# First Fourier stage of the kernels moved into the phases' two banks and ahead of a chunk's sums, in a fused S4D + GLU kernel

## The chip, the cores and the metric

The kernel runs on one core of a Trainium2 chip. A core has TensorE (PE, matmuls), VectorE (DVE), ScalarE (ACT), GpSimd (POOL) and SyncE (SP, which here only starts transfers). Each takes its instructions in the order of its own list, and semaphores make an instruction wait for another engine or for a transfer. The metric is the device time of one execution in microseconds (us); lower is better. Matmul results stand in PSUM, which the program treats as eight banks of 2 KB per partition.

## What is computed

Layer norm of `A_u` (2048 tokens, 448 channels), then two branches added to `A_u`: a state-space convolution over the tokens and a gated MLP (the GLU).

```
xn = layernorm(A_u)
# A: long convolution, one kernel of 2048 taps per channel, built from 256 modes
K  = 2 * Re( sum_n C[d,n] * exp(A[d,n] * dt[d] * l) )          # l = 0..2047
yA = irfft(rfft(K, 4096) * rfft(xn, 4096))[:2048] + xn * D_skip
# B: GLU with sigmoid gate, F = 1792
yB = (sigmoid(xn @ w_gate) * (xn @ w_up)) @ w_down
out = A_u + yA + yB
```

## The kernel before

The program is two Python generators that emit instructions in turn. `glu()` (L731) emits the GLU: for each of 14 blocks of 128 hidden features and each 512 tokens, two groups of 11 gate matmuls (`gate`, L697, matmuls at L710) into PSUM tiles named `gu`, and then the down projection (L831) into tiles `po`. Every operand is split into a high and a low part, so one product is three matmuls. `gu` and `po` tiles come from one pool, `psg`, which hands out four banks in rotation (`tag="gu", bufs=4`). I call gate and down matmuls together the GLU matmuls. The first half of the tokens goes through all blocks, then the second half; between them stand transposes of the second half's tokens, which also use `gu` tiles (the crossing).

`conv()` (L1067) emits the convolution. After a preparation, `kgen` (L455) builds the 448 kernels' values in 56 chunks of 8 channels (NCK = 56), and then `spectra` (L855) does the frequency-domain product and the way back. One chunk `cn` of `kgen` is:

- `ahead(cn + 1)` (L528): two PE matmuls (L535) put the next chunk's phases into `tr`, a PSUM tile of two banks with one buffer; four ACT activations (L543 to L546) turn them into sines and cosines `S` (two buffers).
- `magnitudes` (L490), once per two chunks (a pair): 11 POOL products (L501, L513) into `me` and `mf` (two buffers each); `squares` (L522) on ACT finishes them.
- three DVE products (L603, L604 into `Et`, two buffers; L605 into `Ft`, one buffer).
- the chunk's sums (L619): 32 PE matmuls of `Ft` with `Et` into `ko`, a bank with one buffer that collects four chunks. After the fourth chunk a small matmul (L629) adds the skip term and ACT copies `ko` to `ks` in SBUF (L632).
- the first Fourier stage, `first_stage` (L549), once per four chunks: 32 PE matmuls (L561) of `ks`, even ones into the bank `kp`, odd ones into `kq`. `kp` is a bank of the convolution's pool; `kq` is a bank of the GLU's rotation. Two ACT copies (L567) and a transfer (L568) send the result to DRAM. It is emitted behind the sums of the third chunk of the next four.

So PSUM holds `gu`/`po` x4, `tr` x2, `ko`, `kp`: eight banks. A scheduler of the framework orders each engine's list from the emitted program. `tc.issue_after(glu_mm[0].ins)` puts the sums and the first stage behind the GLU matmul that was emitted last before them. Nothing puts a GLU matmul behind a chunk but the rotation of the four banks, whose third party is `kq`. In `spectra`, from its first step on, GLU matmuls are also put behind the convolution's (`sp_mm`).

Of the kernel before, what the change touches and what calls it, by code (L numbers as in the profile page):

```python
# [11 lines left out]
F32 = mybir.dt.float32  # L12
# [25 lines left out]
HP = 300  # L38
# [14 lines left out]
NCK = D // DC  # L53
# [74 lines left out]
def s4d_glu_kernel(ctx, tc, io):  # L128
    nc = tc.nc
    hp = tc.high_priority  # L130
# [46 lines left out]
    psg = ctx.enter_context(tc.tile_pool(name="psg", bufs=1, space=PSUM))  # L177
# [277 lines left out]
    def kgen(pk):  # L455
# [93 lines left out]
        def first_stage(bank):  # L549

            ks, sk = tl["ks"], tl["sk"].rearrange("p k (s r j) -> p r k s j", r=2, j=2)

            pss = [
                psc[-1].tile([128, 8, 2, 32], F32, name="kp", bufs=1),
                psg.tile([128, 8, 2, 32], F32, name="kq", tag="gu", bufs=4),
            ]
            for s_ in range(8):
                for c in range(2):
                    for r in range(2):
                        rows = slice(64 * r, 64 * r + 64)  # L560
                        nc.tensor.matmul(  # L561
                            pss[r][64 * c : 64 * c + 64, s_].rearrange("p j k -> p (j k)"),
                            ks[rows, s_], wk[rows, c], start=True, stop=True,
                            skip_group_check=True,
                        )
            for r in range(2):
                nc.scalar.copy(sk[:, r], pss[r].rearrange("p s j k -> p k s j"))  # L567
            nc.scalar.dma_start(  # L568
                sk_d[bank // 7, :, :, bank % 7].rearrange("k p c -> p k c"),
                tl["sk"].rearrange("p (k i) c -> p k (i c)", i=4),  # L570
            )
# [11 lines left out]
        for g in range(NCK // NCH):  # L583
            for c in range(NCH):
                cn = g * NCH + c
# [23 lines left out]
                    mags = coming  # L609
                yield WK / 3  # L610
                if cn % 4 == 0:
                    ko = psc[-1].tile([128, 8, 64], F32, name="ko", bufs=1)
                with tc.issue_after(glu_mm[0].ins):
                    for q in range(2):
                        sl = 2 * (cn % 4) + q
# [15 lines left out]
                    )  # L631
                    nc.scalar.copy(ks.rearrange("p s (q b) -> p s q b", q=2), ko.rearrange("p s (b q) -> p s q b", q=2))  # L632
                yield WK / 3
                if cn % 4 == 2 and cn > 3 or cn + 1 == NCK:

                    with hp(HP) if cn + 1 == NCK else tc.issue_after(glu_mm[0].ins):
                        first_stage((cn - 3) // 4 if cn + 1 < NCK else cn // 4)

    def w_load(f, raw=None, eng=nc.sync):
        fs = slice(128 * f, 128 * f + 128)  # L640
# [426 lines left out]
    def conv():  # L1067
        with tc.tile_pool(name="psk", bufs=1, space=PSUM) as ps_, tc.tile_pool(
# [79 lines left out]
            with tc.tile_pool(name="pk", bufs=1, side="right", reuse_waits="tile") as pk:  # L1148
                yield from kgen(pk)
# [8 lines left out]
    lasts, glu_mm, sp_mm, glu_on, outs, x1s, hfs, xls = [], [], [], [], [0], [0], [], []  # L1158
    xq, psc, raws, acl, marks, slots, pqs = list(x_first), [], [], [], [None, None], {}, []
# [44 lines left out]
```

## Time and profile before

| | us |
|---|---|
| median of 3 runs | 746.65 (744.72 to 747.68) |
| the profiled execution | 741.93, of which its span is 740.1 |
| PE busy | 668.2 (90%) |
| DVE busy | 587.9 (79%) |
| ACT busy | 420.6 (57%) |
| POOL busy | 420.8 (57%) |
| granted PE clock, mean | 0.949 |

Busy is the time in which an engine had an instruction running. The clock is the share of full speed that TensorE was granted, so a busy PE at a low clock does less. Matmul rows overlap, since matmuls are pipelined: the distance between starts, not the length of a row, is what one costs. A matmul of 32-bit operands that the program writes as one instruction can stand in the trace as two (the 32 matmuls of a chunk's sums as x64). A row of the chain or of the waits names the waiting instruction, an arrow, and what it waited for.

### The profile page before, as it was taken

To read this page: it belongs to the slowest core of one execution; us is meant where nothing else is said; L and a number is where in the kernel's file an instruction comes from. 1 tells how busy PE (TensorE), PEld (TensorE's weight loads), DVE (VectorE), ACT (ScalarE), POOL (GpSimd) and SP (SyncE) were. 2 spreads that over 40 slices of the span, in tenths; PEclk is the share of its full clock that TensorE was granted. 3 is DMA by queue.
4 is the path that set the end of the run, shared out by engine and by line. 5 is a ranking of instruction groups with operands and counts; after the bars stand their busy time and mean duration, and the time that the engine had idled before them with its cause. 6 is when DMAs were issued, how large, how long until landed. Compare 5 with 4: busy or idle time off the path is not lost.

```text
span 740.1 us, 20863 instructions
## 1 busy us (share of the span) xinstructions
PE 668.2 (90%) x8581; PEld 515.1 (70%) x8581; DVE 587.9 (79%) x779; ACT 420.6 (57%) x651; POOL 420.8 (57%) x453
## 2 busy tenths in 40 slices
PE   2998999988999999788999999999988999788976
PEld 1765878866877787555878888888765667466655
DVE  5799998699999999886679898886757777756833
ACT  3655454689778789887387777777323322222310
POOL 2120116869999999974645776765537773541301
PEclk9999999995999999999999999999998989898987
DMA  9935338451313564354863323322669887874464
GB/s 199 235 114 198 116 102 263 147 188 58 126 48 97 175 191 116 114 181 148 264 188 99 93 95 95 99 81 83 157 171 266 222 244 185 262 210 130 125 169 132
DMA packets 94335, 114.47 MB, mean 155 GB/s; under 512 B 13728, under 2 KB 83936, under 8 KB 93984
## 3 DMA queue, kind: packets, MB, share of 16 engines
q1 hardware_dynamic: 72512, 92.54, 43.1%
q10 hardware_dynamic: 19248, 14.91, 7.0%
q0 software_dynamic: 2480, 5.67, 3.0%
q8 instruction: 68, 1.11, 0.6%
q14 instruction: 27, 0.22, 0.1%
HBM read 68.32 MB, written 44.76 MB: 153 GB/s over the span
## 4 chain that ended last, share of the span: by engine, by line
PE 40%; POOL 19%; issue 11%; DVE 11%; DMA 11%; SPq 5%; ACT 3%; POOLq 0%; DVEq 0%; ACTq 0%
PE gu L710 17%; PE po L831 10%; POOL me L513 7%; PE ko L619 5%; POOL mf L513 5%; PE tr L535 2%; DMA v_d<-vt 2%; POOL dl L796 2%; DVE Ft L605 2%; DVE Et L604 1%; DMA skl<-sk_d 1%; SPq L896 1%; DMA xe<-in_A_u_dram 1%; DVE Et L603 1%; POOL yy L934 1%
## 5 line engine op out<-in xcount | busy, mean ns | idle before, releaser
L513 POOL TENSOR_TENSOR me<-me,pm 128x32 f32<-128x32 f32 (+1 forms) x168 | 149.5, 890 | 67.6 <-DVE Et L604 57.8
L513 POOL TENSOR_TENSOR mf<-mf,pm 128x64 f32<-128x64 f32 (+1 forms) x112 | 118.8, 1061 | 5.3
L710 PE MATMUL gu<-xh,wh 128*128 128x512 f32 x336 | 103.2, 415 | 3.0 <-ACT th L718 1.2
L710 PE MATMUL gu<-xl,wh 128*128 128x512 f32 x336 | 97.7, 394 | 0.0
L710 PE MATMUL gu<-xh,wl 128*128 128x512 f32 x336 | 96.5, 395 | 0.0
L604 DVE TENSOR_TENSOR Et<-me,S 128x1024 f32<-128x1024 f32 x56 | 80.4, 1436 | 13.9 <-ACT me L526 9.0
L831 PE MATMUL po<-dh,hh 128*128 128x448 f32 (+1 forms) x227 | 87.4, 385 | 0.8 <-DVE acc L836 0.8
L605 DVE TENSOR_TENSOR Ft<-mf,S 128x1024 f32<-128x1024 f32 x56 | 83.8, 1496 | 5.1 <-PE ko L619 3.2
L831 PE MATMUL po<-dh,hl 128*128 128x448 f32 (+1 forms) x227 | 84.5, 374 | 2.0 <-DVE hl L728 2.0
L831 PE MATMUL po<-dl,hh 128*128 128x448 f32 (+1 forms) x227 | 84.8, 374 | 0.2 <-POOL dl L796 0.2
L603 DVE TENSOR_TENSOR Et<-me,S 128x1024 f32<-128x1024 f32 x56 | 77.5, 1385 | 4.0 <-ACT S L546 3.5
L710 PEld LDWEIGHTS gu<-xh,wh 128*128 128x128 f32 x336 | 62.6, 195 | 25.8 <-issue 6.9
L543 ACT ACTIVATE S<-tr 128x1024 f32<-128x1024 f32 x56 | 57.9, 1033 | 34.4 <-PE tr L535 18.7
L619 PEld LDWEIGHTS ko<-Et,Ft 128*32 128x32 f32 x3584 | 56.0, 114 | 28.0 <-issue 10.5
L619 PE MATMUL ko<-Et,Ft 128*32 128x64 f32 x3584 | 66.0, 227 | 9.7 <-DVE Ft L605 5.3
L710 PEld LDWEIGHTS gu<-xh,wl 128*128 128x128 f32 x336 | 63.8, 191 | 14.9 <-DVE hl L728 0.7
L710 PEld LDWEIGHTS gu<-xl,wh 128*128 128x128 f32 x336 | 63.0, 189 | 14.8 <-issue 1.4
L726 ACT CAST hh<-gu 128x512 fp32r<-128x512 f32 x56 | 33.1, 591 | 69.8 <-DVE gu L721 68.8
L836 DVE SCALAR_TENSOR_TENSOR acc<-po,acc 128x448 f32<-128x448 f32 (+1 forms) x81 | 48.7, 613 | 28.2 <-PE po L831 27.9
L934 POOL TENSOR_TENSOR yy<-yy 128x448 f32<-128x448 f32 (+1 forms) x16 | 28.5, 1778 | 67.1 <-DVE yy L931 66.9
L546 ACT ACTIVATE S<-S,hpi 128x1024 f32<-128x1024 f32 x56 | 65.6, 1171 | 0.0
L718 ACT ACTIVATE th<-gu 128x512 f32<-128x512 f32 x56 | 33.9, 606 | 43.5 <-PE gu L710 43.5
(214 smaller groups left out, 1346.7 us busy)
## 6 DMA issues: line engine op xcount, KB each, us to landing
sk_d<-sk ACTq DMA_DIRECT2D x14, 512.0 KB
sx<-x_d SPq DMA_DIRECT2D x64, 112.0 KB
skl<-sk_d SPq DMA_DIRECT2D x64, 112.0 KB
v_d<-vt SPq DMA_DIRECT2D x27, 224.0 KB
vp<-v_d SPq DMA_DIRECT2D x6, 896.0 KB
wt_d<-wh SPq DMA_DIRECT2D x9, 512.0 KB
wt_d<-wl SPq DMA_DIRECT2D x9, 512.0 KB
wl<-wt_d SPq DMA_DIRECT2D x9, 512.0 KB
```

What stands on the lines that cost most here:

```text
L513: ins = nc.gpsimd.tensor_tensor(m[:, :, w + a : 2 * w : n], m[:, :, a:w:n], par(base + i).unsqueeze(2).to_broadcast([128, 4 * DC, w // n]) ...
L543: nc.scalar.activation(rows(cs), pv, AF.Abs)
L546: sins[:] = [nc.scalar.activation(cs, cs, AF.Sin, scale=-TWO_PI, bias=hpi)]
L603: v.tensor_tensor(Et[:, :, :, 32:64], two(me[:, :, 32:64]), S[:, 1::-1], ALU.mult)
L604: v.tensor_tensor(Et[:, :, :, 0:32], two(me[:, :, 0:32]), S[:, 1:3, :, ::-1], ALU.mult)
L605: fts[:] = [v.tensor_tensor(Ft, two(mf), S[:, 3:5], ALU.mult)]
L619: nc.tensor.matmul(ko[32 * j : 32 * j + 32, sl], Ft[:, cc, DC * h + 4 * q + j], Et[:, cc, DC * h + 4 * q + j], start=(k == 0), stop=(k == ...
L710: glu_mm[:] = [nc.tensor.matmul(ps, a_, b_, start=(n == 0), stop=(n == len(mm) - 1))]
L718: marks[0] = nc.scalar.activation(th, pgu[0], AF.Tanh, scale=0.5)
L831: glu_mm[:] = [nc.tensor.matmul(po[:, ds], a_[:, bs], w_[:, ds], start=(n == 0), stop=(n == 3 * fc - 1))]
L836: v.scalar_tensor_tensor(acc[:, b, ds], po[:, ds], 0.5, acc[:, b, ds], ALU.mult, ALU.add)
L934: eng.tensor_tensor(yy[:, :, 0], yy[:, :, 0], yy[:, :, 1], ALU.subtract)
```

## The change

`kq` is gone. The first stage writes its two halves to the two banks of a `tr` tile, the tile of the phases. The sums of every second group of four chunks go to the bank `kp` instead of `ko`, so the copy of one group and the sums of the next use different banks. And the first stage is emitted ahead of the third chunk's sums, no longer behind them; the one after the last chunk stays where it was.

```
-            pss = [
-                psc[-1].tile([128, 8, 2, 32], F32, name="kp", bufs=1),
-                psg.tile([128, 8, 2, 32], F32, name="kq", tag="gu", bufs=4),
-            ]
+            both = psc[-1].tile([128, 2, 512], F32, name="tr", bufs=1)
+            pss = [both[:, r].rearrange("p (s j k) -> p s j k", s=8, j=2) for r in range(2)]
...
                 if cn % 4 == 0:
-                    ko = psc[-1].tile([128, 8, 64], F32, name="ko", bufs=1)
+                    ko = psc[-1].tile([128, 8, 64], F32, name=("ko", "kp")[cn // 4 % 2], bufs=1)
+                if cn % 4 == 2 and cn > 3:
+                    with tc.issue_after(glu_mm[0].ins):
+                        first_stage((cn - 3) // 4)
                 with tc.issue_after(glu_mm[0].ins):
...
-                if cn % 4 == 2 and cn > 3 or cn + 1 == NCK:
-
-                    with hp(HP) if cn + 1 == NCK else tc.issue_after(glu_mm[0].ins):
-                        first_stage((cn - 3) // 4 if cn + 1 < NCK else cn // 4)
+                if cn + 1 == NCK:
+                    with hp(HP):
+                        first_stage(cn // 4)
```

In the changed program the line numbers are L620 for the sums, L630 for the skip term, L633 for the copy, L559 for the first stage's matmuls, L565 for its copies.

The scheduler lays the lists out anew. Three places on PE follow. First, before: chunks 2 to 4 near the beginning of `kgen`, in the middle of the GLU's first half. `tr<-sel,ph` are phases, `ko<-Et,Ft` sums.

```order
L710 MATMUL gu<-xl,wh 128x512 x3
L535 MATMUL tr<-sel,ph_1114 128x512 x2
L619 MATMUL ko<-Et_1108,Ft 32x64 x32
L535 MATMUL tr<-sel,ph_1114 128x512 x2
L619 MATMUL ko<-Et_1107,Ft 32x64 x32
L629 MATMUL ko<-dm,ident 128x8
L535 MATMUL tr<-sel,ph_1115 128x512 x2
L619 MATMUL ko<-Et_1108,Ft 32x64 x32
L561 MATMUL kp<-wk,ks 64x64
```

The same place now, chunk 2:

```order
L710 MATMUL gu<-xl,wh 128x512 x3
L831 MATMUL po<-dh,hh 128x448
L831 MATMUL po<-dl,hh 128x448
L535 MATMUL tr<-sel,ph_1114 128x512
L620 MATMUL ko<-Et_1108,Ft 32x64 x32
L535 MATMUL tr<-sel,ph_1114 128x512
L831 MATMUL po<-dh,hl 128x448
L831 MATMUL po<-dh,hh 128x448
L831 MATMUL po<-dl,hh 128x448
```

Before, chunks 2, 3, 4 and 5 follow each other with no GLU matmul between their sums; now 28 stand between the sums of chunks 2 and 3, and 20 to 35 between most others up to chunk 44.

Second, the end of `kgen`. Before, the sums of the last chunk, 55, and what surrounds them:

```order
L831 MATMUL po<-dl,hh 128x448
L831 MATMUL po<-dh,hl 128x448
L619 MATMUL ko<-Et_1107,Ft 32x64 x32
L629 MATMUL ko<-dm,ident 128x8
L831 MATMUL po<-dh,hh 128x448
L831 MATMUL po<-dl,hh 128x448
L831 MATMUL po<-dh,hl 128x448
```

Now, from the last GLU matmul ahead of `spectra` on: the sums of chunks 44 to 47, and the first stage of the group before ahead of the third of them.

```order
L710 MATMUL gu<-xl,wh 128x512 x3
L620 MATMUL kp<-Et_1108,Ft 32x64 x32
L535 MATMUL tr<-sel,ph_1115 128x512 x2
L620 MATMUL kp<-Et_1107,Ft 32x64 x32
L535 MATMUL tr<-sel,ph_1115 128x512 x2
L559 MATMUL tr<-wk,ks 64x64 x32
L620 MATMUL kp<-Et_1108,Ft 32x64 x32
L535 MATMUL tr<-sel,ph_1114 128x512 x2
L620 MATMUL kp<-Et_1107,Ft 32x64 x32
L630 MATMUL kp<-dm,ident 128x8
```

Eight more chunks follow in this way, with no GLU matmul from chunk 44's sums to the first matmuls of `spectra`. Before, 10 to 28 GLU matmuls stood ahead of the sums of nearly each of those chunks, and 45 between chunk 55's sums and `spectra`.

Third, a first stage in the GLU's midst, now (chunk 6):

```order
L710 MATMUL gu<-xh,wl 128x512 x3
L620 MATMUL kp<-Et_1108,Ft 32x64 x5
L559 MATMUL tr<-wk,ks 64x64 x32
L620 MATMUL kp<-Et_1108,Ft 32x64 x27
L710 MATMUL gu<-xr,wl 128x512
L710 MATMUL gu<-xl,wh 128x512 x3
L710 MATMUL gu<-xh,wh 128x512 x3
L710 MATMUL gu<-xr,wh 128x512
L710 MATMUL gu<-xh,wl 128x512 x3
L710 MATMUL gu<-xr,wl 128x512
L710 MATMUL gu<-xl,wh 128x512 x3
L710 MATMUL gu<-xh,wh 128x512 x3
```

and before (the bank ahead of the last), whose halves alternate between `kp` and `kq`:

```order
L831 MATMUL po<-dl,hh 128x448
L831 MATMUL po<-dh,hl 128x448
L561 MATMUL kp<-wk,ks 64x64 x6
L561 MATMUL kq<-wk,ks 64x64 x4
L619 MATMUL ko<-Et_1108,Ft 32x64 x32
```

The next phases, which need the same banks, follow 18 GLU matmuls behind the first stage's end.

The counts over the whole of `kgen`, from the two lists (gate and down matmuls between the starts of two chunks' sums; the 64 transposes and first-stage matmuls of the crossing are counted with the gates):

| from chunk to chunk | before: gate + down | now: gate + down |
|---|---|---|
| 0 to 16 | 179 + 72 | 292 + 144 |
| 16 to 23 | 58 + 72 | 72 + 48 |
| 23 to 35 | 224 + 48 | 241 + 88 |
| 35 to 44 | 126 + 72 | 121 + 104 |
| 44 to 55 | 106 + 108 | 0 |
| 0 to 55 | 693 + 372 | 726 + 384 |
| behind 55, ahead of `spectra` | 33 + 12 | 0 |

From the first matmuls of `spectra` on, the two PE lists hold the same rows.

## Prediction

> **What bounds the kernel now.** I read the cores and the engines' totals first, then the chain of waits, then the busy times by stage, the waits, and at last single rows of the timeline.
>
> ```profile
> core 0: 740.1 us, clock 0.949
> PE 668.2 (90%) x8581; PEld 515.1 (70%) x8581; DVE 587.9 (79%) x779; ACT 420.6 (57%) x651; POOL 420.8 (57%) x453
> ```
>
> PE is the bound over most of the span. To see where it is not, I cut the chunks' stage at the starts of the sums of chunks 0, 16, 23, 35 and 55; the fifth stretch is the seam up to the first matmul of the spectra. The first and the last of the 56 sums in the timeline, and PE's first row behind the seam:
>
> ```profile
> 148.85 1.10 PE L619 MATMUL ko<-Et,Ft 128*32 128x64 f32 x64
> 529.30 0.91 PE L619 MATMUL ko<-Et,Ft 128*32 128x64 f32 x49
> 541.97 0.99 PE L918 MATMUL pk<-skl,tb 64*32 64x224 f32 x32
> ```
>
> The stretches (length, then busy time with the number of instructions of PE, weight loads, DVE, ACT and POOL, then the granted clock):
>
> ```profile
> 148.85:253.39 104.54, 95.39 (x1508) 76.63 (x1508) 102.00 (x102) 85.17 (x122) 94.92 (x88) 0.90 0.37 117
> 253.39:295.99 42.60, 42.39 (x723) 34.71 (x723) 41.79 (x44) 38.18 (x56) 40.56 (x38) 1.00 0.50 145
> 295.99:396.46 100.47, 91.33 (x1296) 65.83 (x1295) 75.38 (x91) 73.78 (x119) 63.81 (x84) 0.97 0.54 171
> 396.46:529.30 132.84, 130.51 (x2061) 108.84 (x2060) 114.28 (x116) 96.28 (x136) 89.11 (x101) 1.00 0.32 98
> 529.30:541.97 12.67, 12.67 (x176) 10.48 (x176) 3.46 (x6) 2.90 (x5) 5.11 (x7) 1.00 0.61 166
> ```
>
> The second and fourth stretches are PE's: next to no idle time, full clock. The first and third lose time. In the first, the list sets chunks 2 to 5 back to back:
>
> ```profile
> 164.87 1.94 PE L619 MATMUL ko<-Et,Ft 128*32 128x64 f32 x64 [1.34 <-DVE Et L603]
> 168.87 1.40 PE L619 MATMUL ko<-Et,Ft 128*32 128x64 f32 x44 [0.26 <-DVE Ft L605]
> 174.84 1.94 PE L619 MATMUL ko<-Et,Ft 128*32 128x64 f32 x64 [2.09 <-DVE Et L603]
> 185.88 1.10 PE L619 MATMUL ko<-Et,Ft 128*32 128x64 f32 x64
> ```
>
> From chunk 2 to chunk 6 that is 21.0 us, 5.25 a chunk. PE waits for products, and the sums take 1.94 us where they take 1.10 elsewhere: at a low clock. This is the pace of chunks without GLU work between them.
>
> **What PE's pieces cost at full clock.** Down and gate matmuls, four starts:
>
> ```profile
> 525.46 0.47 PE L831 MATMUL po<-dh,hh 128*128 128x448 f32 x1
> 529.00 0.37 PE L831 MATMUL po<-dh,hl 128*128 128x448 f32 x1
> 536.89 0.84 PE L710 MATMUL gu<-xh,wh 128*128 128x512 f32 x3
> 539.38 0.84 PE L710 MATMUL gu<-xh,wh 128*128 128x512 f32 x3
> ```
>
> 18 down matmuls: the last starts 3.54 us behind the first, 0.208 each. 11 gate matmuls from 536.89 to 539.38: 0.226 each. With the counts from the lists, the second stretch has 58 gate and 72 down matmuls, 28.1 us of 42.60; the other 14.5 us over 7 chunks make 2.07 a chunk for phases, sums and a quarter of a first stage. The fourth gives (132.84 - 52.4 - 37.4) / 20 = 2.15. I take 2.1. By these prices the first stretch needs 40.5 + 15.0 + 33.6 = 89.1 us and loses 15.4; the third needs 50.6 + 10.0 + 25.2 = 85.8 and loses 14.7 (the crossing, with transposes that wait for DVE and phases that wait for ACT).
>
> **The change part by part.**
>
> *Two banks for the sums.* What could go is PE waiting for the copy of `ko` (L632). PE's waits in the chunks' stage, all that matter:
>
> ```profile
> PE tr L535 <- ACT S L545: 7.8, 7, 2.3
> PE ko L619 <- DVE Ft L605: 5.3, 6, 1.6
> PE ko L619 <- DVE Et L603: 4.2, 3, 2.1
> ```
>
> None is for that copy; phases always lie between a group's last sums and the next group's first. Gain 0. What a copy of a whole bank takes on ACT (shortest, median and longest in ns):
>
> ```profile
> L567 ACT COPY sk<-kp x14: 602/634/662, 183.3 to 533.2; 128x512 f32<-128x512 f32 x14
> ```
>
> The Trainium skill (Perfetto Trace Analysis, Optimizing Tensor Performance, Matmuls) says that independent matmul groups should rotate through PSUM banks so that evacuating one overlaps the next. By that rule 13 copies of 0.63 us, 8 us, would be saved; the waits show nothing to save, so I take 0.
>
> *First stage in `tr`.* The work stays: 448 matmuls, 28 copies, 14 transfers on ACT's list. New are two waits: the first stage for the sines that read `tr`, and the next phases for the two copies, 1.3 us. Behind the waiting phases stand GLU matmuls on PE, and ACT and DVE wait for the phases. In the GLU's midst 18 gate matmuls, 4.1 us, lie between and hide it. In the lone chunks (below) it happens at three first stages; matmuls, copies and phases in a row make up to about 4 us each, 12 in all, if nothing hides them. POOL's pace hides them there, at 12 us for two chunks. I take 0. The first stage ahead of the third sums costs PE nothing: its `ks` was copied two chunks earlier.
>
> *`kq` leaves the GLU's rotation.* This moves most. Before, every first stage took one of the four `gu` banks, so a gate or down group behind it in the rotation could not be listed until the chunks had come that far. That tie of the GLU to the chunks is gone; the tie of the chunks to the GLU remains. The lists show the result: the GLU runs ahead, 1,110 GLU matmuls stand between chunk 0's and chunk 44's sums (726 gate, 384 down), and then chunks 44 to 55 stand alone, where before 1,065 were spread up to chunk 55 and 45 filled the seam.
>
> Chunk 0 starts as before, at 148.85. To chunk 44 PE then needs 726 x 0.226 + 384 x 0.208 + 44 x 2.1 = 164.1 + 79.9 + 92.4 = 336.4 us. To this come losses. Of the first stretch's 15.4 I keep 2, since 27 GLU matmuls and a chunk take PE 8 us, more than POOL or DVE need for a chunk (they filled 94.92 and 102.00 us for 16). Of the crossing's 14.7 I keep 12. Sum 14, with bounds 6 and 24. Chunk 44's sums start at 148.85 + 336.4 + 14 = 499.
>
> Then 11 chunks alone. Who sets their pace? While PE is the bound, POOL is ahead and waits:
>
> ```profile
> POOL me L513 <- DVE Et L604: 57.8, 15, 8.8
> ```
>
> Alone, POOL is the slowest. Three pairs of chunks in the first stretch, from the start of one pair's products to that of the fourth, and one pair in the crossing:
>
> ```profile
> 167.76 2.06 POOL L513 TENSOR_TENSOR me<-me,pm 128x32 f32<-128x32 f32 x3 [4.04 <-DVE Et L604]
> 207.55 0.71 POOL L513 TENSOR_TENSOR me<-me,pm 128x32 f32<-128x32 f32 x2
> 167.76:207.55 39.79, 37.06 (x671) 30.00 (x670) 39.28 (x38) 33.83 (x47) 38.30 (x33) 0.80 0.25 76
> 323.48:333.13 9.65, 8.76 (x125) 5.30 (x123) 8.71 (x12) 9.11 (x17) 9.10 (x11) 1.00 0.59 186
> ```
>
> A pair takes 13.3 us in the first and 9.65 in the second, though DVE is busy in both. What differs is how much of DVE's time goes to the chunks' products (the windows for L603, L604 and L605):
>
> ```profile
> 167.76:207.55 39.79, 9.25 (x7) 0.80 0.25 76
> 167.76:207.55 39.79, 11.83 (x7) 0.80 0.25 76
> 167.76:207.55 39.79, 9.02 (x7) 0.80 0.25 76
> 323.48:333.13 9.65, 1.65 (x1) 1.00 0.59 186
> 323.48:333.13 9.65, 1.21 (x1) 1.00 0.59 186
> ```
>
> The last row stands for L604 and for L605. So 10.0 us of products a pair give 13.3, and 4.1 give 9.65: each us of products adds 0.61. A lone pair has 6 products of 1.43 (30.1 over 21), 8.6 us: 9.65 + 0.61 x 4.5 = 12.4 us. The Trainium skill (SBUF — State Buffer, Who interferes with whom) says that a DVE instruction with two SBUF inputs and a GpSimd instruction that reads SBUF exclude each other for the whole instruction. By that rule a us of products would add a full us, 14.2 a pair, and the sum below would end 7 us later. The trace agrees in kind and gives 0.61; I take that.
>
> When chunk 44's sums start, POOL has the pair 46/47 done or nearly; four pairs remain. It can start the first of them once chunk 45's `Et` is made, about 3 us later (its phases stand 15 gate matmuls ahead of chunk 44's sums; behind them ACT needs 3.9 and two products 2.4). After the last pair come five products and chunk 54's sums, about 7:
>
> ```profile
> 164.91 1.02 ACT L543 ACTIVATE S<-tr 128x1024 f32<-128x1024 f32 x1 [1.38 <-DVE Et L603]
> 167.67 1.18 ACT L546 ACTIVATE S<-S,hpi 128x1024 f32<-128x1024 f32 x1
> 527.31 1.22 DVE L605 TENSOR_TENSOR Ft<-mf,S 128x1024 f32<-128x1024 f32 x1
> ```
>
> So 3 + 4 x 12.4 + 7 = 60 us from chunk 44's to chunk 55's sums, 5.4 a chunk, near the 5.25 of chunks 2 to 6. Bounds: 4 x 9.65 + 10 = 49, and 4 x 13.3 + 10 with half a pair less of lead, 6: 69. Chunk 55's sums start at 499 + 60 = 559, where before it was 529.3: 30 us later.
>
> *The seam.* Behind chunk 55 the way to the spectra is copy, first stage, copies, loads. Before, 45 GLU matmuls lay over it, and the second step still waited for data:
>
> ```profile
> 546.65 0.54 PE L918 MATMUL pk<-skl,t 64*32 64x224 f32 x2 [1.11 <-DMA skl<-sk_d]
> ```
>
> Their 10 us now lie in the sum to chunk 44, and the seam stands idle for about the same 12.7 us, since the second step's loads set its end. So nothing comes back there, and behind it the PE list holds the same rows. The 30 us go through to the end: 741.9 + 30 = 772 in the profiled execution. The runs' median, 746.65, lies 4.7 above the profiled one, so I forecast 746.65 + 30 = 777 for the median.
>
> **Rivals.**
>
> *Not slower.* The loosened order pays: the first stretch's loss goes entirely, and the lone chunks run fast enough. To end where it ended, losses and the lone stretch together must stay under 529.3 - 148.85 - 336.4 = 44 us; with the least loss, 6, that leaves 38 us for 11 chunks. It decides at 3.5 us a chunk, 7 a pair; then the time is 746.7 or a little less. For it: POOL is idle for 57.8 us elsewhere and might have a longer lead. Against it: two buffers of `me` allow no lead beyond one pair, the least seen is 9.65 a pair, and ACT's four activations alone take 3.9 us for a chunk. Chance 0.04.
>
> *Waits in the first 44 chunks.* The new list fits the scheduler's durations, not the chip's. If the sums come too early for their products, PE waits as at 164.87 and 174.84 (1.3 and 2.1 us). Were it 1.3 at each second of 44 chunks, 29 us would come on top: 806. For it: DVE is busy 102.00 of 104.54 us in the first stretch. Against it: the second stretch has DVE at 41.79 of 42.60 and loses nothing at 6.1 us a chunk, and the new list gives 8. Chance 0.14.
>
> **How the numbers follow.** The forecast has 0.82. Its ends: losses 6 with 49 alone give 30 - 8 - 11 = +11, so 758; losses 24 with 69 alone give 30 + 10 + 9 = +49, so 796. Outside lie the two rivals, 0.18. A measurement tells about 0.5% from no change, 3.7 us. Slower by more: 0.82 and 0.14, 0.96. The rival that is not slower gives 0.03 to the same and 0.01 to faster.
>
> **What would show it.** Right: the sums of chunks 45 to 55 follow each other by 5 to 6 us, at a low granted clock, with PE idle for more than half of the time and POOL busy without a break; chunk 44's sums near 499, chunk 55's near 559; chunks 2 to 6 no longer at a low clock; no PE idle time at the copies of `ks`; the spectra as long as before. Wrong: chunk 44 later than 510 (waits among the first chunks), fewer than 4 us a chunk behind it, or a shorter seam and spectra that give time back.

## The result, and the profile after

| | before | after |
|---|---|---|
| median of 4 runs, us | 747.16 (744.72 to 749.35) | 790.5 (779.62 to 793.25) |
| ratio, 95% interval | | 1.0499 (1.0377 to 1.062) |
| profiled execution, us | 741.93 | 789.08 (span 787.3) |

Slower by 43 us in the medians, where 777 was forecast with a range of 758 to 796. The ratio leaves out the two slow runs of the changed kernel (791.92 and 793.25 us) and gives 37 us, and the same kernel run again (e12, below) gives a ratio of 1.0527. The cores and the engines' totals of the changed kernel:

```profile
core 0: 787.3 us, clock 0.914
PE 677.0 (86%) x8581; PEld 525.0 (67%) x8581; DVE 587.8 (75%) x779; ACT 420.5 (53%) x651; POOL 385.5 (49%) x453
```

The work is the same. PE has as many instructions, but it is busy 8.8 us longer and idle for far more. The windows by stage say where: first the stage from chunk 0's sums to the spectra, before and after (length, then busy time of PE, weight loads, DVE, ACT and POOL, then PE's granted clock), each with the part behind it.

```profile
148.85:541.97 393.12, 372.29 (x5759) 296.49 (x5759) 336.91 (x355) 296.32 (x435) 293.51 (x315) 0.97 0.42 129
541.97:740.10 198.13, 167.77 (x2225) 119.08 (x2224) 130.03 (x193) 46.34 (x89) 81.65 (x74) 0.90 0.71 193
```

```profile
149.29:581.85 432.56, 380.01 (x5760) 305.37 (x5760) 335.97 (x356) 296.94 (x436) 259.45 (x315) 0.91 0.38 118
581.85:787.30 205.45, 168.79 (x2224) 119.55 (x2224) 130.11 (x193) 45.59 (x88) 80.19 (x74) 0.87 0.69 186
```

The chunks' stage is 39.4 us longer. PE's idle time in it went from 20.8 to 52.6 us, 31.7 more; the other 7.7 us are the same matmuls running longer at a lower clock. The remaining 7.3 us of the span lie behind it. The same stage cut at the sums of chunks 0, 16, 23, 35, 44 and 55, as in the prediction's sum, with the seam last:

```profile
149.29:278.12 128.83, 127.62 (x1705) 103.67 (x1704) 111.11 (x126) 97.11 (x146) 84.08 (x95) 1.00 0.49 156
278.12:324.87 46.75, 43.96 (x734) 31.49 (x733) 41.80 (x50) 37.75 (x63) 33.48 (x44) 0.93 0.54 174
324.87:431.03 106.16, 99.68 (x1321) 81.94 (x1320) 73.17 (x84) 66.88 (x97) 50.14 (x73) 0.97 0.39 119
431.03:503.93 72.90, 68.97 (x955) 57.48 (x954) 58.58 (x62) 48.10 (x69) 39.00 (x54) 0.98 0.25 71
503.93:569.69 65.76, 35.33 (x920) 26.76 (x920) 51.31 (x36) 45.41 (x61) 52.21 (x51) 0.64 0.18 51
569.69:581.85 12.16, 4.45 (x131) 4.03 (x132) 0.00 (x0) 1.69 (x3) 0.54 (x1) 0.50 0.39 111
```

In the first four stretches PE is busy for 94% of the time or more. In the fifth, the 11 chunks without GLU work, PE is busy for 35.33 of 65.76 us at a clock of 0.64. The seam holds next to nothing but a wait for its loads. The first of the lone sums, and how PE passes through the chunks behind it (start, length, in brackets the wait ahead of it and for whom):

```profile
503.93 1.10 PE L620 MATMUL kp<-Et,Ft 128*32 128x64 f32 x64 [0.46 <-DVE Et L601]
504.96 0.73 PE L535 MATMUL tr<-sel,ph 128*128 128x512 f32 x2
511.14 1.93 PE L620 MATMUL kp<-Et,Ft 128*32 128x64 f32 x64 [5.45 <-DVE Ft L603]
513.00 1.22 PE L535 MATMUL tr<-sel,ph 128*128 128x512 f32 x2
516.75 1.99 PE L559 MATMUL tr<-wk,ks 64*64 64x64 f32 x64 [2.52 <-ACT S L545]
518.66 1.93 PE L620 MATMUL kp<-Et,Ft 128*32 128x64 f32 x64
...
542.53 1.93 PE L620 MATMUL ko<-Et,Ft 128*32 128x64 f32 x64
...
569.69 1.93 PE L620 MATMUL kp<-Et,Ft 128*32 128x64 f32 x64 [1.35 <-DVE Ft L603]
581.85 1.67 PE L918 MATMUL pk<-skl,tb 64*32 64x224 f32 x25 [7.03 <-DMA skl<-sk_d]
```

Most of these sums take 1.93 us instead of 1.10, at the low clock; from 518.66 to 542.53, four chunks, it is 11.9 us a pair. PE waits for DVE's products ahead of eight of the eleven sums behind 503.93. The other three come right behind a first stage, which itself waited for ACT's sines, as at 516.75. These waits, summed over the whole chunks' stage (total, number, longest):

```profile
PE kp L620 <- DVE Ft L603: 10.3, 5, 5.5
PE tr L559 <- ACT S L545: 7.6, 3, 2.5
PE ko L620 <- DVE Et L601: 6.6, 2, 4.9
PE kp L620 <- DVE Et L601: 5.5, 2, 5.0
PE ko L620 <- DVE Ft L603: 5.2, 4, 2.0
```

Of these 35.2 us, 29.5 lie in the lone stretch, where PE is idle for 30.4 in all.

### The profile page after: what moved, and what is told of

The parts are those of the page before. It is cut to its first block, busy times and chain, and to the rows that moved or that the text cites. A ratio compares the mean times of both kernels' runs of the same rounds, so it can differ in the third digit from the quotient of the medians.

```text
span 787.3 us, 20866 instructions
## 1 busy us (share of the span) xinstructions
PE 677.0 (86%) x8581; PEld 525.0 (67%) x8581; DVE 587.8 (75%) x779; ACT 420.5 (53%) x651; POOL 385.5 (49%) x453
## 4 chain that ended last, share of the span: by engine, by line
PE 46%; DMA 13%; DVE 13%; issue 10%; ACT 7%; SPq 6%; POOL 4%; ACTq 0%; DVEq 0%; POOLq 0%
PE gu L710 20%; PE po L831 11%; PE tr L535 4%; PE kp L620 4%; PE ko L620 3%; DMA v_d<-vt 3%; DMA vp<-v_d 2%; DVE Ft L603 2%; PE tr L559 2%; DVE Et L602 2%; DVE Et L601 2%; ACT S L543 2%; SPq L896 1%; ACT S L546 1%; DMA xe<-in_A_u_dram 1%
## 5 line engine op out<-in xcount | busy, mean ns | idle before, releaser
L513 POOL TENSOR_TENSOR me<-me,pm 128x32 f32<-128x32 f32 (+1 forms) x168 | 129.2, 769 | 133.9 <-DVE Et L602 124.3
L603 DVE TENSOR_TENSOR Ft<-mf,S 128x1024 f32<-128x1024 f32 x56 | 84.5, 1508 | 42.5 <-ACT S L546 35.7
L513 POOL TENSOR_TENSOR mf<-mf,pm 128x64 f32<-128x64 f32 (+1 forms) x112 | 106.4, 950 | 5.8
L710 PE MATMUL gu<-xh,wh 128*128 128x512 f32 x336 | 105.0, 421 | 4.4 <-ACT xh L217 2.9
L543 ACT ACTIVATE S<-tr 128x1024 f32<-128x1024 f32 x56 | 57.9, 1033 | 68.9 <-PE tr L535 56.7
L602 DVE TENSOR_TENSOR Et<-me,S 128x1024 f32<-128x1024 f32 x56 | 77.0, 1375 | 9.6 <-ACT me L526 5.6
L601 DVE TENSOR_TENSOR Et<-me,S 128x1024 f32<-128x1024 f32 x56 | 75.7, 1351 | 10.2 <-ACT S L546 8.8
L934 POOL TENSOR_TENSOR yy<-yy 128x448 f32<-128x448 f32 (+1 forms) x16 | 26.7, 1667 | 79.3 <-DVE yy L931 79.3
L544 ACT ACTIVATE S<-tr 128x1024 f32<-128x1024 f32 x56 | 57.6, 1029 | 0.0
L721 DVE SCALAR_TENSOR_TENSOR gu<-th,gu 128x512 f32<-128x512 f32 x56 | 38.6, 688 | 24.2 <-PE gu L710 14.5
```

What stands on the lines that cost most here:

```text
L513: ins = nc.gpsimd.tensor_tensor(m[:, :, w + a : 2 * w : n], m[:, :, a:w:n], par(base + i).unsqueeze(2).to_broadcast([128, 4 * DC, w // n]) ...
L543: nc.scalar.activation(rows(cs), pv, AF.Abs)
L544: nc.scalar.activation(rows(S[:, 0:5:4]), pv, AF.Sin, scale=TWO_PI)
L601: v.tensor_tensor(Et[:, :, :, 32:64], two(me[:, :, 32:64]), S[:, 1::-1], ALU.mult)
L602: v.tensor_tensor(Et[:, :, :, 0:32], two(me[:, :, 0:32]), S[:, 1:3, :, ::-1], ALU.mult)
L603: fts[:] = [v.tensor_tensor(Ft, two(mf), S[:, 3:5], ALU.mult)]
```

## The experiments

In all of them the GLU's matmuls, the sums and the spectra are the same work; what differs is named. (e5 and e9 leave out some of POOL's products, e6 and e9 add matmuls.) "Alone" names the chunks, two or more in a row, that have no GLU matmul in PE's list between their sums and those of the chunk before. Each ratio is to runs of the kernel before on the same chip.

| kernel | alone | median, us | ratio to before, 95% |
|---|---|---|---|
| before | 3 to 5 | 747.16 | 1 |
| the change | 45 to 55 | 790.5 | 1.0499 (1.0377 to 1.062) |
| e1 | 47 to 55 | 779.27 | 1.0432 (1.037 to 1.0495) |
| e2 | 3, 4, 53 to 55 | 791.48 | 1.06 (1.0543 to 1.0658) |
| e3 | 54, 55 | 761.3 | 1.0198 (1.0143 to 1.0254) |
| e4 | 43, 44 | 765.0 | 1.0242 (1.0196 to 1.0288) |
| e5 | 45 to 55 | 780.73 | 1.0479 (1.0412 to 1.0545) |
| e6 | 45 to 55 | 779.69 | 1.0478 (1.0422 to 1.0534) |
| e7 | 47 to 55 | 780.19 | 1.0486 (1.0417 to 1.0555) |
| e8 | 47 to 55 | 783.57 | 1.053 (1.0467 to 1.0593) |
| e9 | 45 to 55 | 777.18 | 1.0427 (1.039 to 1.0464) |
| e10 | none | 756.42 | 1.0132 (1.0089 to 1.0175) |
| e11 | none | 753.82 | 1.0102 (1.0068 to 1.0135) |
| e12, the change again | 45 to 55 | 785.64 | 1.0527 (1.0483 to 1.0571) |

**Which part of the change costs: e1, e7, e8.** The theory on trial: `kq` in the GLU's rotation held the GLU back, and losing that tie is the whole cost. Rivals: the first stage's new place, or banks that now collide.

e8 is the kernel before with one line changed:

```
-                psg.tile([128, 8, 2, 32], F32, name="kq", tag="gu", bufs=4),
+                psc[-1].tile([128, 2, 512], F32, name="tr", bufs=1)[:, 1].rearrange(...),
```

> The kernel before with one line changed: the first stage's second half (kq) lies in the second bank of tr and no longer in the GLU's rotation of four banks; its first half stays in kp, there is one sum bank, and the first stage stays behind the sums. The GLU's matmuls run ahead in PE's row as in the changed kernel: none is left for chunks 47 to 55 and for the seam. List theory (what costs is that kq no longer ties the GLU to the chunks): 10 lone chunks as in e1, 774 to 788 us. Rival (the cost lies in the new place of the first stage, or in kp's leaving to the sums, or in tr being shared by both halves with the phases): 743 to 755 us.

783.57 us: the list theory holds. That one line gives a slowdown as large as the whole change's, with one sum bank, `kp` kept, and the first stage behind the sums. (Nine sums had no GLU matmul ahead, and a tenth had 15; the expectation rounds that to ten.) The stage of e8, to be read against the first row of before above, and in it the stretch from chunk 46's to chunk 55's sums:

```profile
147.05:575.02 427.97, 398.93 (x5759) 317.84 (x5759) 326.50 (x355) 296.60 (x436) 256.86 (x315) 0.92 0.38 119
509.84:562.93 53.09, 35.23 (x757) 27.18 (x756) 39.70 (x28) 36.00 (x50) 34.18 (x39) 0.57 0.21 58
```

The lone chunks are as slow here as in the changed kernel, which took 51.03 us from chunk 46's to chunk 55's sums. The line does two things, though: it takes `kq` out of the GLU's rotation, and it puts a half of the first stage into the phases' banks. e8 alone can't part them; e3, below, bounds the second.

e1 has both halves in `tr`, but one sum bank and the old place:

```
 (the changed kernel, with)
-                    ko = psc[-1].tile([128, 8, 64], F32, name=("ko", "kp")[cn // 4 % 2], bufs=1)
+                    ko = psc[-1].tile([128, 8, 64], F32, name="ko", bufs=1)
 (and first_stage called behind the sums, as before)
```

> One part alone: the first stage writes to the phases' two banks, so no GLU bank is used by it; one bank for the sums and the old place of the first stage stay. The GLU again runs ahead in the PE list: chunks 46 to 55 stand alone, ten instead of eleven. List theory (the time is the price of lone chunks, about 3.9 us each over the 2.1 us that a chunk costs PE, plus some us at the seam): 780 to 792 us, as the whole change. Bank theory (it is the sharing of banks and the first stage's place ahead of the third sums that cost): this has only the sharing, so about half of the loss, 765 us or less. Rotation theory (the second bank for the sums is worth some us): slower than the whole change by about 8 us.

779.27 us, 0.7 below the list theory's range and far from the bank theory's; nor is it slower than the whole change, as the rotation theory asked. Place and second sum bank are not needed for the cost. e7 adds the second sum bank to e1 and nothing else:

```
-                    ko = psc[-1].tile([128, 8, 64], F32, name="ko", bufs=1)
+                    ko = psc[-1].tile([128, 8, 64], F32, name=("ko", "kp")[cn // 4 % 2], bufs=1)
```

> The kernel of e1 (first stage in the two banks of tr, one sum bank, at the place that it has before) with the second sum bank added: ko and kp in turn for each four chunks. The order of every engine's row is otherwise that of e1, 10 lone chunks included. The forecast's own step: the second bank is worth nothing, since ACT's copy of the sums is not what sums wait for, so 777 to 782 us, beside e1's 779.27. The rule that the two halves of a rotation let PE write while the other is read, priced in the forecast at 8 us: 769 to 774.

780.19 us. The second bank gains nothing: by the ratios e7 lies 0.5% above e1 with intervals that overlap, where the rotation rule asked for about 8 us, 1.1%, below.

**Putting the tie back, or holding the GLU in another way: e2, e3, e4.** e2 leaves only the first half in `tr` and puts the second back into the GLU's rotation, with two sum banks at the old place:

```
-            pss = [both[:, r].rearrange("p (s j k) -> p s j k", s=8, j=2) for r in range(2)]
+            pss = [
+                both[:, 0].rearrange("p (s j k) -> p s j k", s=8, j=2),
+                psg.tile([128, 8, 2, 32], F32, name="kq", tag="gu", bufs=4),
+            ]
 (and first_stage called behind the sums, as before)
```

> Banks as in the change for the sums and for one half of the first stage; its other half goes to a bank of the GLU's rotation again, and its place is the old one. The list is tied again: a few lone chunks at the start as before, three at the end, 39 GLU matmuls in the seam. List theory: 3 lone chunks of 3.9 us more than before, 752 to 762 us, so the rotating bank is what held the GLU back. Bank theory (phases wait for the first stage's copies and the first stage for the sines): still 775 us or more, since half of the first stage shares the phases' banks.

791.48 us: a miss. The tie does spread the GLU again, but the scheduler parts the two halves of the first stage and sets the `kq` half right behind the group's last sums, where its input is not there yet:

```profile
482.95 0.73 PE L535 MATMUL tr<-sel,ph 128*128 128x512 f32 x2 [1.30 <-ACT S L545]
484.76 1.15 PE L562 MATMUL kq<-wk,ks 64*64 64x64 f32 x32 [1.07 <-ACT ks L633]
...
487.04 0.57 PE L832 MATMUL po<-dl,hh 128*128 128x448 f32 x1
487.42 0.57 PE L832 MATMUL po<-dh,hl 128*128 128x448 f32 x1
...
490.15 0.36 PE L832 MATMUL po<-dl,hh 128*128 128x448 f32 x1
490.35 0.37 PE L832 MATMUL po<-dh,hl 128*128 128x448 f32 x1
```

Behind two waits of little over 1 us the down matmuls follow each other by 0.38 us, and by 0.20 some 3 us later: a short gap costs twice, as idle time and as a slow spell behind it. Over the stage, with as many matmuls as before, PE is busy 404.17 us instead of 372.29:

```profile
148.28:586.23 437.95, 404.17 (x5760) 320.75 (x5759) 322.80 (x356) 296.00 (x435) 251.06 (x315) 0.93 0.38 116
```

PE's waits for that copy ahead of the `kq` half come to 4.3 us in four places, so this fault is a part of e2's cost; what makes up the rest is not shown. e2 is therefore no clean test of the tie, since it brought a fault of its own. It does show that spreading the GLU by itself is not enough.

e3 keeps the whole change and holds the GLU's matmuls behind the sums of the chunk that was emitted six before (`sum_mm` collects the last matmul of each chunk's sums):

```
+    def behind():
+        if glu_on:
+            return tc.issue_after(sp_mm[0].ins)
+        return tc.issue_after(sum_mm[-6].ins) if len(sum_mm) >= 6 else nullcontext()
...
-            with tc.issue_after(sp_mm[0].ins) if glu_on else nullcontext():
+            with behind():
```

> The whole change, and one rule more: a GLU matmul is put behind the sums of the sixth last chunk that was emitted, so that the GLU cannot run further ahead. Two to three chunks stand alone at the end instead of eleven. No bank moves and no instruction is added. List theory: the start of the chunks' stage loses nothing as in the change, some 2.5 lone chunks cost 10 us, the unfilled seam 10: 745 to 757 us. Bank theory: nothing of the banks or the first stage's place has changed, so 780 us or more.

761.3 us. The direction is as expected: 2.0% over the kernel before, where the change has 5.0 to 5.3%. The size missed by 4 us at least. Every bank and the first stage's place are those of the change here, so in this order the sharing of the phases' banks costs at most these 2.0%; the rest of the slowdown is the order's. e4 is the same with the lead cut from six to four behind chunk 36 and to two behind chunk 46, so that 29 GLU matmuls are left for the seam:

```
+        n = 6 if len(sum_mm) < 36 else 4 if len(sum_mm) < 46 else 2
+        return tc.issue_after(sum_mm[-n].ins) if len(sum_mm) >= n else nullcontext()
```

> As the run before it, but the allowed lead shrinks: six chunks, four from chunk 36 on, two from chunk 46 on. No chunk at the end stands alone, two do in the middle, and 29 GLU matmuls are left for the seam. List theory: 8 us for lone chunks, nothing lost at the start, most of the seam filled: 735 to 748 us, no slower than the kernel before the change and perhaps faster. Bank theory: 780 us or more.

765.0 us: a miss of 17, and no better than e3; what holds e4 up stays open. Why holding the GLU doesn't give everything back shows in the windows of e3, cut at the sums of chunks 0, 16, 32, 47, and the spectra:

```profile
147.58:257.10 109.52, 104.11 (x1590) 86.20 (x1589) 104.29 (x111) 87.58 (x127) 92.21 (x91) 1.00 0.45 143
257.10:381.30 124.20, 114.60 (x1656) 81.12 (x1655) 99.29 (x111) 94.11 (x148) 77.05 (x99) 0.89 0.49 152
381.30:491.60 110.30, 110.30 (x1617) 91.94 (x1616) 84.58 (x97) 73.88 (x107) 58.94 (x83) 1.00 0.32 101
491.60:555.74 64.14, 45.44 (x903) 37.49 (x903) 41.99 (x38) 39.50 (x56) 40.58 (x44) 0.91 0.28 80
```

In the third stretch PE is never idle. But the crossing (the second) is idle for 9.6 us and runs at 0.89. And in the last stretch 18.7 us are idle, the last lone chunks and a seam without GLU work.

**What sets the pace of the lone chunks: e5, e6, e9.** The prediction had POOL's products. The chain of waits of the changed kernel has no POOL row in it at all; by line, from 518 to 566:

```profile
by line: PE tr L535 14.6%; ACT S L543 12.8%; PE ko L620 11.9%; PE kp L620 11.9%; PE tr L559 8.9%; DVE Ft L603 8.6%; ACT S L544 7.7%; DVE Et L601 5.2%; DVE Et L602 5.2%; ACT S L545 4.6%; ACT S L546 4.3%; issue 4.1%; DVEq L603 0.1%
```

That is a ring: PE's phases, ACT's sines, DVE's products, PE's sums, and again phases. Yet POOL was busy 44.74 us of 47.75 in eight of these chunks:

```profile
511.14:558.89 47.75, 26.64 (x660) 19.84 (x660) 37.01 (x24) 32.11 (x43) 44.74 (x44) 0.64 0.14 38
```

e5 takes away much of POOL's work there; it leaves out the doubling products of `mf` for chunks 48 to 55:

```
-            for m, base, nst in ((me, 0, 6), (mf, 7, 5)):
+            for m, base, nst in ((me, 0, 6), (mf, 7, 5)) if b < 24 else ((me, 0, 6),):
```

> The changed kernel without POOL's products of the magnitudes' second factor (mf, L513) for chunks 48 to 55; their output columns are therefore wrong, and nothing else changes: the 11 lone chunks stay, and PE's row is the same. In the changed kernel the lone stretch (sums of chunk 44 to sums of chunk 55) took 65.76 us, POOL took about 12 us for each pair of chunks in it, and so did a pass round PE, ACT and DVE. POOL theory (the forecast's: POOL's products set the pace of the lone chunks): POOL's share of a pair falls to about 7 us, the stretch goes to 45 to 52 us, and the time to 771 to 778 us. Ring theory (the chain PE at half clock, ACT's copies and sines, DVE's products, PE again sets the pace): the stretch stays at 62 to 66 us, a little of it gained where DVE no longer shares with POOL, and the time at 785 to 793.

e6 keeps PE's clock up with matmuls whose results nobody reads:

```
+            if cn > 45:
+                idle = psc[-1].tile([128, 512], F32, name=("kp", "ko")[(cn - 1) // 4 % 2], bufs=1)
+                with tc.issue_after(mm.ins):
+                    for _ in range(8):
+                        extra = nc.tensor.matmul(idle, ph[:, cn % 2, 0:128], sel, start=True, stop=True)
+                dummy[:] = [extra]
...
-                with tc.issue_after(glu_mm[0].ins):
+                with tc.issue_after((dummy or glu_mm)[0].ins), tc.issue_after(glu_mm[0].ins):
```

(`mm` is the last matmul of the phases. The last line puts the chunk's sums behind the added matmuls.)

> The changed kernel with 8 added matmuls (128x512, results never read) behind the phases of each chunk from 46 on, written to the idle one of the two sum banks, so that PE is not idle in the lone stretch; nothing else changes. 8 x 0.22 us at full clock is 1.8 us for each chunk, and a lone chunk had 6.0 us of which PE was busy 3.2 at half clock. Ring theory: if the granted clock rises to 0.9 or more, PE's part of a pass falls by half, about 1.3 us a chunk, so the stretch of 65.76 us goes to 50 to 58 us and the time to 775 to 783; if the clock stays near 0.64, the added matmuls lengthen the pass and the time is 795 to 810. POOL theory: with the clock up the stretch stays at 63 to 67 us, since POOL still needs 12 us a pair, and the time stays at 786 to 793.

e9 has both edits.

> The edits of e5 and e6 together: the changed kernel without POOL's products of the magnitudes' second factor (mf, L513) for chunks 48 to 55, and with the 8 added matmuls behind the phases of each chunk from 46 on. From the sums of chunk 46 to those of chunk 55 the changed kernel took 51.0 us, e5 47.7 and e6 48.0. Theory of two limits (POOL's products and the ring of PE, ACT and DVE take nearly the same time, so that taking one away uncovers the other): with both eased the stretch falls by clearly more than the two gains added, to 36 to 43 us, and the time to 764 to 775. Rival (a third thing sets the pace, such as ACT's or DVE's own work): the gains add at most, 43.5 to 47 us, and the time is 775 to 783.

The stretch from chunk 46's to chunk 55's sums, in the change and in e5, e6 and e9:

```profile
518.66:569.69 51.03, 28.58 (x728) 21.53 (x724) 39.10 (x27) 35.83 (x48) 37.95 (x36) 0.63 0.20 58
```

```profile
518.50:566.20 47.70, 26.70 (x734) 20.32 (x729) 32.98 (x27) 35.71 (x48) 16.95 (x22) 0.72 0.21 59
```

```profile
516.90:564.90 48.00, 33.56 (x800) 25.24 (x796) 37.30 (x27) 35.48 (x48) 41.05 (x37) 0.98 0.22 61
```

```profile
518.51:563.00 44.49, 33.26 (x788) 25.21 (x788) 34.41 (x27) 34.66 (x48) 18.77 (x22) 0.99 0.21 61
```

Taking away more than half of POOL's busy time (37.95 to 16.95 us) gains 3.3 us. Raising the clock from 0.63 to 0.98 gains 3.0. Both together gain 6.5, the two added. (The same stretch of the unaltered kernel in e12 took 50.7 us, so these gains are clear of the difference between those two executions.) So each of the two simple theories missed its number: for the whole lone stretch e5 measured 59.6 us from 506.6 to 566.2, and e6 61.3 from 503.54 to 564.85, both between the theories' ranges. My theory of two limits missed too: it asked for clearly more than the sum of the two. What holds is the rival of e9. With PE at full clock and POOL eased, the chain of e9 from 518.5 to 563 goes mostly over ACT and DVE (its lines behind the phases stand 6 later, so L607 to L609 are L601 to L603):

```profile
by line: DVE Et L607 15.1%; DVE Ft L609 12.8%; ACT S L549 9.2%; PE tr L535 7.8%; ACT S L550 7.7%; PE kp L626 7.4%; ACT S L552 7.0%; issue 6.6%; DVE Et L608 5.6%; ACT me L526 5.5%; PE ko L626 4.9%; ACT S L551 4.6%; PE ko L542 4.2%; ACT ks L6
```

In e6 alone, with the clock up but POOL whole, the chain (518 to 566) goes over POOL instead:

```profile
by line: POOL me L513 38.0%; POOL mf L513 33.9%; POOL mf L501 8.1%; issue 8.0%; DVE Ft L609 4.9%; DVE Et L607 2.7%; PE kp L626 2.4%; DVE Et L608 2.4%; POOLq L513 0.2%; POOLq L1019 0.0%
```

All of them lie close: 44.49 us for 9 chunks is 4.9 a chunk without POOL's and the clock's part, and 5.7 with both. A chunk that stands alone costs about what the passage PE, ACT, DVE, PE takes, and neither easing POOL nor raising the clock saved more than some 3 us of 51. Easing ACT or DVE was not tried. The totals of e5, e6 and e9 differ from the change's by little more than their intervals; it is the stretches that tell them apart.

**Does filling the chunks that stood alone before pay: e10, e11.** The kernel before loses 15.4 us around its chunks 2 to 6. e10 takes nothing of the change, and holds the GLU behind the sums of the chunk emitted two before; e11 four before.

```
+        return tc.issue_after(sum_mm[-2].ins) if len(sum_mm) >= 2 else nullcontext()
 (in e11 with 4 for 2)
```

> The kernel before, with the GLU's matmuls issued behind the sums of the chunk issued two before; nothing of the change is in it. In PE's row 408 GLU matmuls stand before chunk 0's sums instead of 483, and the chunks 3 to 5, which had none, have 13 to 22. Theory (chunks without GLU matmuls cost what PE idles in them; the kernel before lost 15.4 us in chunks 1 to 6): 8 to 15 us faster, 730 to 738. Rival (chunk 0 is not ready earlier, so PE idles for the 75 GLU matmuls taken away ahead of it, or the loss comes back at the next chunks): 744 to 752.

> As e10 with the lead four chunks: 452 GLU matmuls before chunk 0's sums, and 11, 22, 22, 11, 7 in chunks 1 to 5. Theory: 6 to 14 us faster than the kernel before, 731 to 740, and not behind e10 if chunk 0 isn't ready as early as e10 wants it. Rival: 744 to 752.

756.42 and 753.82 us, slower than before by 1.3% and 1.0%: both theories missed, mine by sign. Part of it is the first half of the rival. Ahead of chunk 0's sums, before and then e10:

```profile
0.00:148.85 148.85, 128.13 (x599) 99.58 (x600) 120.94 (x231) 77.96 (x129) 45.66 (x64) 0.98 0.63 171
```

```profile
0.00:144.86 144.86, 112.65 (x526) 86.52 (x526) 116.05 (x226) 73.77 (x121) 39.67 (x54) 0.94 0.62 167
144.86:553.47 408.61, 391.48 (x5832) 311.88 (x5832) 341.77 (x361) 300.31 (x441) 292.81 (x326) 0.97 0.41 127
```

PE has 15.5 us less to do there, but chunk 0 starts only 4.0 us earlier. The chunks' stage, which then holds these 75 GLU matmuls too, is 15.5 us longer than the 393.12 of before. At the prediction's 0.226 us each they need 17.0, so of the 15.4 us lost around the lone chunks hardly more than 1 came back. The remaining 4.2 us lie behind the first matmul of the spectra (202.3 us against 198.1). For e11, the stretches from chunk 0's to chunk 16's and on to chunk 32's sums; of before the second alone (the first stands in the prediction: 104.54 us), then e11's two:

```profile
253.39:375.00 121.61, 112.39 (x1690) 83.42 (x1689) 100.29 (x114) 93.79 (x146) 91.71 (x102) 0.97 0.55 168
```

```profile
143.69:254.30 110.61, 102.06 (x1543) 81.22 (x1543) 98.73 (x104) 85.80 (x123) 100.01 (x94) 0.96 0.35 112
254.30:382.38 128.08, 117.20 (x1685) 87.55 (x1684) 96.47 (x116) 93.67 (x148) 76.67 (x97) 0.92 0.52 160
```

In e11 the first stretch holds 34 GLU matmuls more, about 7.4 us, and is 6.1 us longer: with no chunk alone it loses nearly as much as the kernel before. PE's idle time there is 8.6 us instead of 9.2, no longer in chunks 2 to 6 but spread. The second holds practically the same GLU work (334 matmuls instead of 337) and is 6.5 us longer, at a clock of 0.92 instead of 0.97. So giving those chunks GLU work did not take their loss away; POOL and DVE are busy for about nine tenths of that first stretch or more either way. What makes the crossing longer in e11 is not settled.

**The same kernel again: e12.**

> The changed kernel once more, unaltered, for a second profiled execution. In the first, the part from the first matmul of the spectra to the end took 205.45 us, where it took 198.13 before, with the same rows in PE's list. Theory (that part varies from one execution to the next and the change does nothing to it): another value between 199 and 206, as the kernels with the same rows there gave (199.0 to 206.4), while chunk 44's sums come at 501 to 507 and the lone stretch takes 63 to 67 us again; time 779 to 792. Rival (the change costs 7 us behind chunk 55): 204 to 207 again.

785.64 us. Its chunk 44 came at 505.09, and its lone stretch took 63.4 us. The part behind the seam:

```profile
580.79:786.00 205.21, 165.07 (x2224) 118.19 (x2224) 130.00 (x193) 45.55 (x88) 80.13 (x74) 0.89 0.68 186
```

205.21 us fits both expectations. e9, whose list has the same rows there behind the same seam, took 199.00:

```profile
575.30:774.30 199.00, 163.97 (x2224) 116.88 (x2224) 130.73 (x193) 46.15 (x88) 81.70 (x74) 0.91 0.69 192
```

So the 7 us behind the seam are seen twice in the changed kernel, but not in every kernel with that list; and e10, which has nothing of the change, took 202.3 there. Whether they belong to the change stays open.

## Why the prediction was right, and where it was off

- **Two sum banks: 0.** Right (e7). The Trainium skill (Perfetto Trace Analysis, Optimizing Tensor Performance, Matmuls) has independent groups rotate through banks, and the prediction's estimate by that rule was 8 us saved. No run shows any of it: what sums wait for here is DVE's products and not a bank.
- **`kq` out of the GLU's rotation moves most.** Right. e8 has it in one line, 1.053 (1.0467 to 1.0593), and e3, which holds the GLU back and moves no bank, has 1.0198.
- **Chunk 44's sums at 499.** 503.93 in the first execution, 505.09 in the second. By the prediction's prices the losses were 18.3 us instead of 14. The start's fell from 15.4 to none (128.83 us where the prices give 129.5; the prediction kept 2). The crossing, chunks 16 to 35, lost 14.0 (it kept 12), and 5.0 came from chunks 35 to 44, which had none in the sum. Inside its bounds of 6 and 24.
- **The lone chunks take 60 us, by POOL's pace.** 65.76, inside the bounds of 49 and 69, but this is the step that was off, in size and in reason. The pace was met: 47.75 us for eight chunks, 11.9 a pair, where 12.4 was forecast. But that was in part luck. POOL was not alone the slowest: the passage through PE at a clock of 0.63, ACT and DVE happens to take about as long, and the chain goes that way, with POOL nowhere on it. With POOL much eased the stretch lost only 3.3 us (e5). The ends were not met: 7.2 us to chunk 45's sums and 10.8 behind chunk 53's, 18.0 where 3 + 7 were put.
- **Full exclusion of DVE and POOL.** By the rule in the Trainium skill (SBUF — State Buffer, Who interferes with whom) the prediction's estimate was 14.2 us a pair, and by the trace's slope of 0.61 it was 12.4. The 11.9 measured tests neither, since POOL is not on the chain there. e6 comes nearer to a test, since its chain goes mostly over POOL: from chunk 46's sums (516.94) to chunk 54's (561.45) it took 11.1 us a pair. That is less than either estimate, and the slope was the better one. e5's DVE does become faster when POOL does less: 39.10 to 32.98 us of busy time for the same 27 instructions.
- **First stage in `tr`: 0, hidden by POOL.** Not hidden. PE waited for the sines ahead of it at three places of the lone stretch, 2.5 us each time, as at 516.75, and L559 has 8.9% of the chain there. This time lies inside the pace measured above and is not added again; e8, whose first stage stands behind the sums, is no faster.
- **The seam gives nothing back.** Right: 12.16 us against 12.67, its end set by the loads (7.03 us of wait at 581.85).
- **The 30 us go through to the end.** 39.9 us were there at the first matmul of the spectra (581.85 against 541.97), and 7.3 more came behind it. The lone chunks' ends, the losses and that last part are the whole distance between 30 and 47 us in the profiled executions.
- **The rivals.** Not slower: needed 3.5 us a chunk or less; it was 6.0. Waits in the first 44 chunks: chunk 44 would have come later than 510; it came at 503.93.
- **What would show it.** As written came the low clock (0.64), chunk 44's sums, full clock for the first chunks, and no waits of sums or phases for the copies of `ks`. Not as written: the sums followed each other by 3.3 to 7.5 us, on average 6.0, and not by 5 to 6; PE was idle for 46% of the lone stretch, not more than half; POOL was busy for 52.21 of 65.76 us, not without a break; chunk 55's sums came at 569.69, not near 559; and the spectra were 7.3 us longer, not as long as before.

## What to carry to other kernels

Where two streams of work share a rotation of buffers, the rotation can also be what keeps them in step. Taking one stream out of it can let the scheduler run the other ahead, and here the stream with the long passage through several engines was then left alone at the end, at a low clock and with nothing between its steps. Before freeing such a buffer, compare the orders of the two lists and count what is left beside the slow stream; and don't expect to repair it by a lead alone, since e3 and e4 got back about three of the five per cent and no kernel here beat the one before.

## What the runs showed of the hardware that was not expected

A single small DVE instruction took as long as POOL's products ran without a break. Of DVE and POOL in the changed kernel, shortly before the lone stretch:

```profile
485.23 4.58 DVE L449 SCALAR_TENSOR_TENSOR pm<-pm 128x128 f32<-128x128 f32 x1
```

```profile
485.44 0.62 POOL L513 TENSOR_TENSOR me<-me,pm 128x256 f32<-128x256 f32 x1
...
488.61 1.05 POOL L513 TENSOR_TENSOR mf<-mf,pm 128x512 f32<-128x512 f32 x1
```

The same DVE instruction takes 0.39 us elsewhere:

```profile
479.93 0.39 DVE L449 SCALAR_TENSOR_TENSOR pm<-pm 128x128 f32<-128x128 f32 x1
```

It ended at 489.8, just behind POOL's row of products (489.7). In e12 it took 4.56 us and again ended with POOL's products, and in the changed kernel none of the 25 instructions of that line that overlap no work of POOL took more than 0.29. The rows agree in kind with the exclusion that the Trainium skill describes (SBUF — State Buffer, Who interferes with whom); no run here isolates it. The other surprise is the price of short gaps on PE: in e2 two waits of 1.30 and 1.07 us were followed by some 3 us of matmuls at nearly half pace. And in e6, with 8 added matmuls a chunk, the clock was 0.98 in the lone stretch, where it was 0.63 without them.
